# A long convolution by DFT matmuls and an MLP on one core: LayerNorm moved into the forward transform, keys and values multiplied out of PSUM, squares and diagonals spread over engines

## The chip, the core and the metric

The kernel runs on one core of a Trainium2 chip. The core has a matrix engine (TensorE, "PE" in the profile), a vector engine (VectorE, "DVE"), an activation engine (ScalarE, "ACT"), GpSimd ("POOL") and a sync engine (SyncE, "SP") that here only issues DMAs. Matmuls write into PSUM, which has eight banks; a tile of 128x512 float32 fills one. The metric is the device time of the launch in microseconds (us).

## The reference, cut to what matters

```python
def A(q, k, v, shift_k, ssm_k, ssm_D):              # S = 2048, D = 512
    k_shift = sum(k delayed by t * shift_k[:, 3 - t] for t in range(4))   # written short
    kv = k_shift * v
    y = irfft(rfft(kv, 2S) * rfft(ssm_k, 2S))[:S]    # causal convolution along S, per channel
    y = y + kv * ssm_D
    return q * y

def B(x, w1, w2, w3, w4):                            # F = 1792
    h = gelu(layernorm(x) @ w1)
    hs = (four quarters of h, shifted by +1, -1, +2, -2 along S) @ w2
    x1 = x + hs
    return x1 + gelu(layernorm(x1) @ w3) @ w4

x = A_q
h = x + A(layernorm(x), A_k, A_v, A_shift_k, A_ssm_k, A_ssm_D)
out = h + B(layernorm(h), w1, w2, w3, w4)
```

All inputs and the output are bfloat16.

## The kernel before

Most tiles hold a transposed activation: 128 partitions of channels, DC = 4 groups of channels, S = 2048 positions. NB = 16 blocks of 128 positions, NW = 4 windows of 512 positions.

The convolution is done with cosine and sine matrices that the kernel makes itself. `gen_trig` makes them: three VectorE instructions for the angle, folded into one turn, and three on ScalarE.

```python
def gen_trig(pool, x0, g, j0, cw, out_sin, out_cos, gmax):
    e = pool.tile([P, gmax, cw], F32, tag="ge");  t = pool.tile([P, gmax, cw], F32, tag="gt")
    ...
    nc.vector.tensor_tensor(out=ev, in0=bj_b, in1=rv_b, op=MUL)                 # L107
    nc.vector.tensor_scalar(out=tv, in0=ev, scalar1=MAGIC, scalar2=MAGIC, op0=ADD, op1=SUB)  # L108
    nc.vector.tensor_tensor(out=tv, in0=ev, in1=tv, op=SUB)                     # L110
    nc.scalar.activation(out_sin, tv, ACT.Sin, scale=TWO_PI)                    # L111
    nc.scalar.activation(ev, tv, ACT.Abs)                                       # L112
    nc.scalar.activation(out_cos, ev, ACT.Sin, bias=halfpi, scale=-TWO_PI)      # L113
```

LayerNorm over channels (which lie on partitions): sums and sums of squares by matmuls with a column of ones, then 1/std and -mean/std per position are put on diagonals (`dga`, `dgb`), spread over all partitions by a matmul with a matrix of ones, copied out of PSUM, and applied. It is called for q ("qn"), for h with two outputs ("hn") and for x1 ("ln1").

```python
def layernorm_feat(xt, yt, name, yt2=None):
    ...
    lps = ...tile_pool(bufs=2, space=PSUM)
    sq = lq.tile([P, DC, S], BF16)
    nc.vector.tensor_tensor(out=sq[:], in0=xt[:], in1=xt[:], op=MUL)            # L121
    pst = lps.tile([P, NB, 2], F32, bufs=1)
    for blk in range(NB):
        for c in range(DC): matmul(pst[:, blk, 0:1], lhsT=xt[:, c, blk], rhs=ones_col)   # L126
        for c in range(DC): matmul(pst[:, blk, 1:2], lhsT=sq[:, c, blk], rhs=ones_col)   # L129
    nc.scalar.mul(stat, pst, 1.0 / D)                                           # L132
    ...                                        # variance, square root (L139), rstd, brow
    for (acol, bcol, ydst) in scales:
        for w in range(NW):
            psbc = lps.tile([P, 1024], F32)
            for j in range(4):
                nc.vector.tensor_scalar_mul(dga, ident, acol[:, blk:blk + 1])   # L163, dga: 2 buffers
                nc.vector.tensor_scalar_mul(dgb, ident, bcol[:, blk:blk + 1])   # L165, dgb: 2 buffers
                matmul(psbc[:, j * P:(j + 1) * P], lhsT=ones_pp, rhs=dga)       # L166
                matmul(psbc[:, 512 + j * P:512 + (j + 1) * P], lhsT=ones_pp, rhs=dgb)   # L168
            nc.scalar.copy(abc, psbc[:, 0:512]);  nc.scalar.copy(bbc, psbc[:, 512:1024])  # L172, L173
            for c in range(DC):
                nc.vector.tensor_tensor(out=tn, in0=xt[:, c, lo:hi], in1=abc, op=MUL)     # L177
                nc.vector.tensor_tensor(out=ydst[:, c, lo:hi], in0=tn, in1=bbc, op=ADD)   # L178
```

The front loads k and v transposed, shifts k, multiplies, and transposes the product back block by block:

```python
kT = kvg.tile([P, DC, S], BF16);  vT = kvg.tile([P, DC, S], BF16)
for c in range(DC): nc.sync.dma_start_transpose(kT[:, c, :], A_k[0, :, c * P:(c + 1) * P])     # L203
for c in range(DC): nc.scalar.dma_start_transpose(vT[:, c, :], A_v[0, :, c * P:(c + 1) * P])   # L205
for c in range(DC):
    nc.vector.tensor_scalar_mul(ksh, kT[:, c, :], ssk[:, c, 0:1])               # L208
    for j in range(1, 4): nc.vector.scalar_tensor_tensor(out=ksh[:, j:], ...)   # L210
    nc.vector.tensor_tensor(out=kvTc, in0=ksh, in1=vT[:, c, :], op=MUL)         # L214
    for b in range(NB):
        pt = psK.tile([P, P], BF16)
        nc.tensor.transpose(pt, kvTc[:, b * P:(b + 1) * P], ident)              # L217
        (nc.scalar.copy if b % 2 == 0 else nc.vector.tensor_copy)(kv_all[:, b, c * P:(c + 1) * P], pt)  # L220, L222
for lb in range(NB): nc.sync.dma_start_transpose(hf[:, lb, :], A_ssm_k[...])     # L225
for c in range(DC): nc.sync.dma_start_transpose(xT[:, c, :], A_q[...])           # L228
layernorm_feat(xT, qnT, "qn")
gen_trig(..., nyq_s, nyq)
```

The forward transform has 16 chunks of 128 frequencies and one last frequency. Four spectra (real and imaginary of kernel and of kv), each with two PSUM buffers of one bank, are summed over the 16 blocks, copied out and combined into `Qr`, `Qi`:

```python
for ci, (f0, cw) in enumerate(fchunks):
    cs, ss = ...                                       # gen_trig, one chunk of 128 columns, 2 buffers
    akr, aki, ghr, ghi = four psA tiles
    for b in range(NB):
        matmul(ghr, lhsT=cs[:, b], rhs=hf[:, b]);  matmul(akr, lhsT=cs[:, b], rhs=kv_all[:, b])   # L258, L259
        matmul(ghi, lhsT=ss[:, b], rhs=hf[:, b]);  matmul(aki, lhsT=ss[:, b], rhs=kv_all[:, b])   # L260, L261
    nc.scalar.copy(acr, akr); ... aci, gcr, gci        # L266 to L269
    ...                                                # 8 VectorE instructions: Qr[:, q], Qi[:, q]
```

The inverse transform runs over four windows; the strips of sines come in groups of four frequency blocks:

```python
for w in range(NW):
    yps = psI.tile([P, DC, 512], F32)                  # four banks, 2 buffers
    for qg in range(0, NB, GQ):                        # GQ = 4
        iss, ics = its tiles (2 buffers);  gen_trig(itf, qg, GQ, lo, 512, iss, ics, GQ)
        for qi in range(GQ):
            for c in range(DC):
                matmul(yps[:, c], lhsT=Qr[...], rhs=ics[:, qi])    # L319
                matmul(yps[:, c], lhsT=Qi[...], rhs=iss[:, qi])    # L321
    ...                                                # last frequency, L324
    for c in range(DC):
        nc.vector.tensor_tensor(out=ty, in0=yps[:, c], in1=qnT[:, c, lo:hi], op=MUL)   # L328
        nc.vector.tensor_tensor(out=hT[:, c, lo:hi], in0=ty, in1=xT[:, c, lo:hi], op=ADD)   # L330
```

Then come the LayerNorms of h, the matmuls with w1 and w2 (whose results x1T are written channel group by channel group, L386), the LayerNorm of x1, and the MLP with w3 and w4 window by window.

Of the kernel before, what the change touches and what calls it, by code (L numbers as in the profile page):

```python
# [34 lines left out]
def kernel(  # L35
# [79 lines left out]
    def layernorm_feat(xt, yt, name, yt2=None):  # L115
        with ExitStack() as lctx:
            lp = lctx.enter_context(tc.tile_pool(name=f"lnp_{name}", bufs=2))
            lq = lctx.enter_context(tc.tile_pool(name=f"lnq_{name}", bufs=1))
            lps = lctx.enter_context(tc.tile_pool(name=f"lps_{name}", bufs=2, space=bass.MemoryType.PSUM))
            sq = lq.tile([P, DC, S], BF16, tag="sq")  # L120
            nc.vector.tensor_tensor(out=sq[:], in0=xt[:], in1=xt[:], op=MUL)  # L121
# [35 lines left out]
            for (acol, bcol, ydst) in scales:  # L157
                for w in range(NW):
                    psbc = lps.tile([P, 1024], F32, tag="psbc")
                    for j in range(4):  # L160
                        blk = 4 * w + j
                        dga = lp.tile([P, P], BF16, tag="dga")
                        nc.vector.tensor_scalar_mul(dga[:], ident[:], acol[:, blk:blk + 1])  # L163
                        dgb = lp.tile([P, P], BF16, tag="dgb")
                        nc.vector.tensor_scalar_mul(dgb[:], ident[:], bcol[:, blk:blk + 1])  # L165
                        nc.tensor.matmul(psbc[:, j * P:(j + 1) * P], lhsT=ones_pp[:, :],  # L166
                                         rhs=dga[:], start=True, stop=True)
                        nc.tensor.matmul(psbc[:, 512 + j * P:512 + (j + 1) * P], lhsT=ones_pp[:, :],  # L168
                                         rhs=dgb[:], start=True, stop=True)
# [11 lines left out]
    nyq_s = pI.tile([1, 1, S], BF16)  # L181

    with ExitStack() as pa_ctx:
# [12 lines left out]
        with ExitStack() as kvctx:  # L196
            kvg = kvctx.enter_context(tc.tile_pool(name="kvg", bufs=1))
            kvt = kvctx.enter_context(tc.tile_pool(name="kvt", bufs=1))
            psK = kvctx.enter_context(tc.tile_pool(name="psK", bufs=2, space=bass.MemoryType.PSUM))
            kT = kvg.tile([P, DC, S], BF16)  # L200
            vT = kvg.tile([P, DC, S], BF16)
            for c in range(DC):
                nc.sync.dma_start_transpose(kT[:, c, :], A_k[0, :, c * P:(c + 1) * P])  # L203
            for c in range(DC):
                nc.scalar.dma_start_transpose(vT[:, c, :], A_v[0, :, c * P:(c + 1) * P])  # L205
            for c in range(DC):
                ksh = kvt.tile([P, S], BF16, tag="ksh")
# [5 lines left out]
                kvTc = kvt.tile([P, S], BF16, tag="kvTc")  # L213
                nc.vector.tensor_tensor(out=kvTc[:], in0=ksh[:], in1=vT[:, c, :], op=MUL)  # L214
                for b in range(NB):
                    pt = psK.tile([P, P], BF16, tag="pt")
                    nc.tensor.transpose(pt[:], kvTc[:, b * P:(b + 1) * P], ident[:])  # L217
                    eng = nc.scalar if (b % 2 == 0) else nc.vector
                    if eng is nc.scalar:
                        nc.scalar.copy(kv_all[:, b, c * P:(c + 1) * P], pt[:])  # L220
                    else:
                        nc.vector.tensor_copy(kv_all[:, b, c * P:(c + 1) * P], pt[:])  # L222
# [7 lines left out]
        layernorm_feat(xT, qnT, "qn")  # L230
        with ExitStack() as ny_ctx:
            nyp = ny_ctx.enter_context(tc.tile_pool(name="nyp", bufs=1))
            gen_trig(nyp, NB, 1, 0, S, nyq_s[0:1, 0:1, :], nyq[0:1, 0:1, :], 1)
# [3 lines left out]

        for ci, (f0, cw) in enumerate(fchunks):
            if ci == 0:
                cs, ss = cs_pre, ss_pre  # L240
            else:
                cs = strips.tile([P, NB, CW], BF16, tag="cs")
                ss = strips.tile([P, NB, CW], BF16, tag="ss")
                gen_trig(tmpf, 0, NB, f0, cw, ss[:, :, :cw], cs[:, :, :cw], NB)
            if cw > 1:
                nq = cw // P
                for qi in range(nq):
                    q = f0 // P + qi
                    akr = psA.tile([P, 512], F32, tag="akr")
                    aki = psA.tile([P, 512], F32, tag="aki")  # L250
                    ghr = psA.tile([P, 512], F32, tag="ghr")
                    ghi = psA.tile([P, 512], F32, tag="ghi")
                    for b in range(NB):
# [4 lines left out]
                        nc.tensor.matmul(ghr[:], lhsT=lhs_c, rhs=hf[:, b, :], start=st, stop=sp)  # L258
                        nc.tensor.matmul(akr[:], lhsT=lhs_c, rhs=kv_all[:, b, :], start=st, stop=sp)  # L259
                        nc.tensor.matmul(ghi[:], lhsT=lhs_s, rhs=hf[:, b, :], start=st, stop=sp)  # L260
                        nc.tensor.matmul(aki[:], lhsT=lhs_s, rhs=kv_all[:, b, :], start=st, stop=sp)  # L261
                    acr = combp.tile([P, 512], BF16, tag="acr")
                    aci = combp.tile([P, 512], BF16, tag="aci")
                    gcr = combp.tile([P, 512], BF16, tag="gcr")
                    gci = combp.tile([P, 512], BF16, tag="gci")
                    nc.scalar.copy(acr[:], akr[:])  # L266
                    nc.scalar.copy(aci[:], aki[:])
                    nc.scalar.copy(gcr[:], ghr[:])
                    nc.scalar.copy(gci[:], ghi[:])  # L269
# [16 lines left out]
            else:  # L286
                akr = psA.tile([P, 512], F32, tag="akr")
                ghr = psA.tile([P, 512], F32, tag="ghr")
                for b in range(NB):
                    st = (b == 0)  # L290
                    sp = (b == NB - 1)
                    nc.tensor.matmul(ghr[0:1, :], lhsT=cs[:, b, 0:1], rhs=hf[:, b, :], start=st, stop=sp)
                    nc.tensor.matmul(akr[0:1, :], lhsT=cs[:, b, 0:1], rhs=kv_all[:, b, :], start=st, stop=sp)
                acr = combp.tile([P, 512], BF16, tag="acr")
                gcr = combp.tile([P, 512], BF16, tag="gcr")
                nc.scalar.copy(acr[0:1, :], akr[0:1, :])
                nc.scalar.copy(gcr[0:1, :], ghr[0:1, :])
                p1 = combp.tile([P, 512], BF16, tag="p1")
                nc.vector.tensor_tensor(out=p1[0:1, :], in0=acr[0:1, :], in1=gcr[0:1, :], op=MUL)
                nc.vector.tensor_scalar_mul(Qr[0:1, 16, :], p1[0:1, :], 1.0 / L)  # L300

    with ExitStack() as pi_ctx:
# [5 lines left out]
        GQ = 4  # L308
        for w in range(NW):
            lo, hi = w * 512, (w + 1) * 512  # L310
            yps = psI.tile([P, DC, 512], F32, tag="yps")
            for qg in range(0, NB, GQ):
                iss = its.tile([P, GQ, 512], BF16, tag="iss")
                ics = its.tile([P, GQ, 512], BF16, tag="ics")
                gen_trig(itf, qg, GQ, lo, 512, iss[:], ics[:], GQ)
# [139 lines left out]
```

## Time and profile before

| | |
|---|---|
| time, median of 4 runs | 714.63 us (713.75 to 715.33) |
| span of the profiled run | 713.4 us |
| instructions | 7378 |
| PE busy | 545.8 us (76%) |
| DVE busy | 526.8 us (74%) |
| ACT busy | 339.0 us (48%) |
| POOL busy | 2.9 us |

A busy share is a mean over stages of different kinds. The stages follow one another: the front (loads, shifted k, LayerNorm of q) until the first forward matmul at 101.2 us; the forward transform until 331; the inverse transform from 343.5 to 460.5; the LayerNorms of h until the first matmul with w1 near 507; w1 and w2 until 551.8; the LayerNorm of x1 until the first matmul with w3 near 577; the MLP to the end. In the lines of the profile "L217" is a line of the kernel, "out<-in" are tile names, and the text in brackets says how long the engine had been idle before an instruction and what released it.

### The profile page before, as it was taken

What the parts mean: (1) busy time and instruction counts of PE and PEld (TensorE: products, weight loads), DVE (VectorE), ACT (ScalarE), POOL (GpSimd) and SP (SyncE); (2) the same over time, 40 slices, a digit from 0 to 9 for tenths busy, and PEclk for the clock granted to TensorE, in tenths of its full rate; (3) what the DMA queues carried; (4) which work ended last, traced back from release to release, by engine and by line L of the source; (5) the groups of instructions that cost most, each with busy time, mean ns of one, the idle gap of its engine ahead of it and who ended that gap; (6) DMA issues with size and microseconds to landing.
All of it is one profiled execution on the core that took longest, in us unless ns stands there. A gap on an engine that the chain in (4) does not pass through costs nothing.

```text
span 713.4 us, 7378 instructions
## 1 busy us (share of the span) xinstructions
PE 545.8 (76%) x2800; PEld 245.0 (34%) x2800; DVE 526.8 (74%) x1000; ACT 339.0 (48%) x391; POOL 2.9 (0%) x11
## 2 busy tenths in 40 slices
PE   0122459999999999995799999833558468999976
PEld 0011324444444444442344444331223323433422
DVE  4699693756756665615989997179887778888984
ACT  0333417466456446512978787112470256445460
POOL 1000000000000000000000000000000000000000
PEclk9999999999999999998799999955699569999996
DMA  5646000000000000000000000070000000000000
GB/s 118 126 102 125 1 1 0 1 1 0 1 1 0 1 1 0 1 1 0 0 1 1 0 1 1 0 266 0 1 0 0 2 0 0 31 1 29 1 30 30
DMA packets 39925, 15.68 MB, mean 22 GB/s; under 512 B 34513, under 2 KB 39378, under 8 KB 39890
## 3 DMA queue, kind: packets, MB, share of 16 engines
q1 hardware_dynamic: 29234, 10.76, 6.2%
q10 hardware_dynamic: 10656, 4.46, 2.5%
q8 instruction: 22, 0.36, 0.2%
q14 instruction: 13, 0.11, 0.1%
HBM read 4.72 MB, written 2.10 MB: 10 GB/s over the span
## 4 chain that ended last, share of the span: by engine, by line
PE 57%; DVE 24%; ACT 11%; DMA 5%; issue 3%; SPq 0%; ACTq 0%; DVEq 0%
PE yps L319 8%; PE yps L321 8%; PE ghr L258 8%; PE akr L259 8%; PE ghi L260 8%; PE aki L261 8%; ACT xs L336 4%; DVE u L338 3%; PE po L412 3%; ACT sg L343 3%; DMA vT<-in_A_v_dram 2%; DVE tn L177 2%; DVE g_sb L344 2%; DVE u L339 2%; DVE ksh L210 2%
## 5 line engine op out<-in xcount | busy, mean ns | idle before, releaser
L319 PE MATMUL yps<-ics,Qr 128*128 128x512 bf16 x256 | 98.4, 384 | 12.1 <-ACT ics L113 12.1
L112 ACT ACTIVATE e<-t 128x2048 f32<-128x2048 f32 (+2 forms) x34 | 63.0, 1854 | 80.3 <-DVE t L110 79.9
L321 PE MATMUL yps<-iss,Qi 128*128 128x512 bf16 x256 | 98.3, 384 | 0.0
L260 PE MATMUL ghi<-hf,ss 128*128 128x512 bf16 x240 | 91.1, 380 | 0.0
L261 PE MATMUL aki<-kv_all,ss 128*128 128x512 bf16 x240 | 91.0, 379 | 0.0
L258 PE MATMUL ghr<-hf,cs 128*128 128x512 bf16 x240 | 91.0, 379 | 0.0
L259 PE MATMUL akr<-kv_all,cs 128*128 128x512 bf16 x240 | 91.0, 379 | 0.0
L107 DVE TENSOR_TENSOR e<-bj,rv 128x2048 f32<-128x2048 f32 (+2 forms) x34 | 75.7, 2226 | 16.6 <-ACT cs L113 11.8
L110 DVE TENSOR_TENSOR t<-e,t 128x2048 f32<-128x2048 f32 (+2 forms) x34 | 75.8, 2228 | 1.0
L412 PE MATMUL po<-g_sb,w_sb 128*128 128x512 bf16 x224 | 63.8, 391 | 9.2 <-DVE g_sb L344 5.6
L217 PE MATMUL pt<-ident,kvTc 128*128 128x128 bf16 x64 | 14.1, 275 | 62.6 <-DVE kvTc L214 29.8
L405 PE MATMUL pg<-ln1T,w_sb 128*128 128x512 bf16 x224 | 58.3, 394 | 3.6 <-ACT bbc L173 1.2
L272 DVE TENSOR_TENSOR p<-acr,gcr 128x512 bf16<-128x512 bf16 x16 | 6.8, 425 | 71.1 <-ACT acr L266 56.4
L343 ACT ACTIVATE sg<-u 128x512 bf16<-128x512 bf16 x72 | 45.2, 631 | 24.6 <-DVE u L341 23.0
L166 PE MATMUL psbc<-dga,ones_pp 128*128 128x128 bf16 x64 | 17.2, 269 | 44.8 <-DVE dga L163 44.8
L336 ACT CAST xs<-pg 128x512 bf16<-128x512 f32 x56 | 32.6, 583 | 36.4 <-DVE g_sb L344 20.9
L108 DVE TENSOR_SCALAR t<-e 128x2048 f32<-128x2048 f32 (+2 forms) x34 | 40.6, 1194 | 1.9
L113 ACT ACTIVATE ics<-e,halfpi 128x2048 bf16<-128x2048 f32 x16 | 32.0, 2003 | 20.7 <-PE yps L319 20.7
L338 DVE TENSOR_TENSOR u<-xs 128x512 bf16<-128x512 bf16 x72 | 30.5, 423 | 13.7 <-ACT xs L336 13.0
L321 PEld LDWEIGHTS <-Qi 128*128 128x128 bf16 x256 | 25.3, 99 | 42.4 <-DVE t L110 11.9
L319 PEld LDWEIGHTS <-Qr 128*128 128x128 bf16 x256 | 25.3, 99 | 32.5 <-issue 3.3
L405 PEld LDWEIGHTS <-w_sb 128*128 128x128 bf16 x224 | 22.2, 99 | 37.9 <-issue 17.8
(124 smaller groups left out, 836.8 us busy)
## 6 DMA issues: line engine op xcount, KB each, us to landing
out_dram<-osb SPq DMA_DIRECT2D x16, 128.0 KB, 1.8
w_sb<-in_B_w_dram SPq DMA_DIRECT2D x1, 1792.0 KB, 8.6
w_sb<-in_B_w_dram ACTq DMA_DIRECT2D x1, 1792.0 KB, 15.2
w_sb<-in_B_w_dram SPq DMA_DIRECT2D x1, 512.0 KB, 12.5
w_sb<-in_B_w_dram ACTq DMA_DIRECT2D x1, 512.0 KB, 16.1
hf<-in_A_ssm_k_dram SPq DMA_TRANSPOSE x16, 2.7
vT<-in_A_v_dram ACTq DMA_TRANSPOSE x4, 4.2
kT<-in_A_k_dram SPq DMA_TRANSPOSE x4, 4.2
```

The source lines that it names most:

```text
L107: nc.vector.tensor_tensor(out=ev, in0=bj_b, in1=rv_b, op=MUL)
L110: nc.vector.tensor_tensor(out=tv, in0=ev, in1=tv, op=SUB)
L112: nc.scalar.activation(ev, tv, ACT.Abs)
L258: nc.tensor.matmul(ghr[:], lhsT=lhs_c, rhs=hf[:, b, :], start=st, stop=sp)
L259: nc.tensor.matmul(akr[:], lhsT=lhs_c, rhs=kv_all[:, b, :], start=st, stop=sp)
L260: nc.tensor.matmul(ghi[:], lhsT=lhs_s, rhs=hf[:, b, :], start=st, stop=sp)
L261: nc.tensor.matmul(aki[:], lhsT=lhs_s, rhs=kv_all[:, b, :], start=st, stop=sp)
L319: nc.tensor.matmul(yps[:, c, :], lhsT=Qr[:, q, c * P:(c + 1) * P], rhs=ics[:, qi, :], start=(q == 0), stop=False)
L321: nc.tensor.matmul(yps[:, c, :], lhsT=Qi[:, q, c * P:(c + 1) * P], rhs=iss[:, qi, :], start=False, stop=False)
L343: nc.scalar.activation(sg[:], u[:], ACT.Sigmoid)
L405: nc.tensor.matmul(pg[:], lhsT=w3_sb[:, k, k2 * P:(k2 + 1) * P], rhs=ln1T[:, k, lo:hi], start=(k == 0), stop=(k == DC - 1))
L412: nc.tensor.matmul(po[:], lhsT=w4_sb[:, k2, m * P:(m + 1) * P], rhs=g_sb[:, k2, :], start=(k2 == 0), stop=(k2 == FC - 1))
```

## The change

It has eight parts. (1) v is no longer loaded transposed; it is loaded in its own layout, block by block, and the shifted k is transposed on TensorE and multiplied by v as it leaves PSUM. That takes four transposing loads and the evicting copies away. (2) The LayerNorm of q moves from ahead of the forward transform to chunk 6 of it, so that it can run beside matmuls; its PSUM pool gets one buffer, to fit. (3) To make room in PSUM the forward transform does the spectra of the kernel (`gh`) first and those of kv (`ak`) after them, each a tile of two banks, two in all. (4) The first strip of the inverse transform is made at the end of the forward stage into tiles of its own. (5) The squares of the LayerNorms are cut into pieces of 512 columns, and (6) those of h, except the last window, go to GpSimd. (7) `dgb` is made on ScalarE. (8) The last frequency's unused sine tile `nyq_s` goes; sine and cosine are written to one tile.

```diff
-            lps = ...tile_pool(name=f"lps_{name}", bufs=2, space=PSUM)
+            lps = ...tile_pool(name=f"lps_{name}", bufs=(1 if name == "qn" else 2), space=PSUM)
             sq = lq.tile([P, DC, S], BF16, tag="sq")
-            nc.vector.tensor_tensor(out=sq[:], in0=xt[:], in1=xt[:], op=MUL)
+            for w in range(NW):
+                for c in range(DC):
+                    eng = nc.gpsimd if (name == "hn" and w < NW - 1) else nc.vector
+                    eng.tensor_tensor(out=sq[:, c, w * 512:(w + 1) * 512], in0=xt[:, c, w * 512:(w + 1) * 512],
+                                      in1=xt[:, c, w * 512:(w + 1) * 512], op=MUL)
 ...
-                        nc.vector.tensor_scalar_mul(dgb[:], ident[:], bcol[:, blk:blk + 1])
+                        nc.scalar.mul(dgb[:], ident[:], bcol[:, blk:blk + 1])
 ...
-    nyq_s = pI.tile([1, 1, S], BF16)
+    GQ = 4
+    iss0 = pI.tile([P, GQ, 512], BF16)
+    ics0 = pI.tile([P, GQ, 512], BF16)
 ...
+            vtp = kvctx.enter_context(tc.tile_pool(name="vtp", bufs=3))
-            vT = kvg.tile([P, DC, S], BF16)
-            for c in range(DC):
-                nc.scalar.dma_start_transpose(vT[:, c, :], A_v[0, :, c * P:(c + 1) * P])
 ...                                            # ksh as before, but one tile for each c (kshs)
-                nc.vector.tensor_tensor(out=kvTc[:], in0=ksh[:], in1=vT[:, c, :], op=MUL)
-                for b in range(NB): ...        # transpose of kvTc, copy to kv_all
+            for b in range(NB):
+                vt = vtp.tile([P, D], BF16, tag="vt")
+                nc.scalar.dma_start(vt[:], A_v[0, b * P:(b + 1) * P, :])
+                pt = psK.tile([P, DC, P], BF16, tag="pt")
+                for c in range(DC):
+                    nc.tensor.transpose(pt[:, c, :], kshs[c][:, b * P:(b + 1) * P], ident[:])
+                nc.vector.tensor_tensor(out=kv_all[:, b, :], in0=pt[:, :, :], in1=vt[:, :], op=MUL)
 ...
-        layernorm_feat(xT, qnT, "qn")
 ...
+            if ci == 6 and not qn_done:
+                layernorm_feat(xT, qnT, "qn")
+                qn_done = True
 ...                                            # akr, aki, ghr, ghi: two tiles of two banks, tag "spec", bufs=2
+                    gh = psA.tile([P, 2, 512], F32, tag="spec")
+                    for b in range(NB): ...    # gh[:, 0] (cs), gh[:, 1] (ss) with hf
+                    nc.scalar.copy(gcr[:], gh[:, 0, :]);  nc.scalar.copy(gci[:], gh[:, 1, :])
+                    ak = psA.tile([P, 2, 512], F32, tag="spec")
+                    for b in range(NB): ...    # ak[:, 0] (cs), ak[:, 1] (ss) with kv_all
+                    nc.scalar.copy(acr[:], ak[:, 0, :]);  nc.scalar.copy(aci[:], ak[:, 1, :])
 ...
+        gen_trig(tmpf, 0, GQ, 0, 512, iss0[:], ics0[:], GQ)
 ...
-                iss = its.tile(...);  ics = its.tile(...);  gen_trig(itf, qg, GQ, lo, 512, iss[:], ics[:], GQ)
+                if w == 0 and qg == 0:
+                    iss, ics = iss0, ics0
+                else:
+                    iss = its.tile(...);  ics = its.tile(...);  gen_trig(itf, qg, GQ, lo, 512, iss[:], ics[:], GQ)
```

## The prediction

> **What bounds the kernel now.** I read the page first: busy shares and the 40 slices.
>
> ```profile
> PE 545.8 (76%) x2800; PEld 245.0 (34%) x2800; DVE 526.8 (74%) x1000; ACT 339.0 (48%) x391; POOL 2.9 (0%) x11
> ...
> PE   0122459999999999995799999833558468999976
> PEld 0011324444444444442344444331223323433422
> DVE  4699693756756665615989997179887778888984
> ```
>
> TensorE and VectorE are both near three quarters, and they take turns. The row of PE is 9 in two long blocks (the two transforms) and low in the first six slices and in slices 27 to 34, where the row of DVE is high. So I cut the span at the ends of the stages and asked for busy time in each stretch (columns: stretch, length, busy PE, PEld, DVE, ACT, POOL with counts, clock, DMA share, GB/s).
>
> ```profile
> 0.00:102.00 102.00, 24.24 (x227) 13.44 (x228) 78.93 (x135) 29.51 (x52) 2.73 (x9) 1.00 0.41 83
> 102.00:331.00 229.00, 229.00 (x1054) 102.83 (x1053) 134.84 (x179) 116.31 (x112) 0.00 (x0) 1.00 0.00 1
> 331.00:344.00 13.00, 0.93 (x4) 0.34 (x3) 12.42 (x9) 7.33 (x6) 0.00 (x0) 0.62 0.00 0
> 344.00:460.50 116.50, 116.41 (x528) 51.12 (x526) 94.73 (x67) 84.06 (x45) 0.00 (x0) 0.98 0.00 1
> 460.50:511.00 50.50, 18.67 (x201) 11.12 (x202) 43.54 (x146) 11.07 (x22) 0.14 (x2) 0.53 0.28 94
> 511.00:551.80 40.80, 28.31 (x122) 11.55 (x121) 33.10 (x80) 19.28 (x32) 0.00 (x0) 0.99 0.00 0
> 551.80:581.00 29.20, 12.94 (x169) 7.99 (x169) 22.15 (x71) 6.73 (x13) 0.00 (x0) 0.57 0.01 1
> ```
>
> The reader is to see: a front of 102 us with VectorE busy 79; a forward transform of 229 us in which TensorE never stops while VectorE has 94 us free; a hole of 13 us; an inverse transform with TensorE full again; and two LayerNorms of 50 and 29 us with VectorE busy most of the time and TensorE at a little over half clock. Work that leaves the front or the LayerNorms, or moves under the forward transform, is worth its whole length; work taken off VectorE inside the transforms is worth nothing by itself.
>
> The waits tell what ends the front (waiter, releaser: us, times, longest):
>
> ```profile
> PE pt L217 <- DVE kvTc L214: 29.8, 4, 21.2
> ...
> PE ghr L258 <- ACT bbc L173: 1.5, 1, 1.5
> ...
> SPq L203 <- DMA vT<-in_A_v_dram: 23.1, 4, 6.6
> ```
>
> The first forward matmul (L258, at 101.2 in the timeline) waits for the last copy of the LayerNorm of q (L173), although it needs nothing of it: it needs the banks of PSUM that this LayerNorm held. The queue of SyncE waits for transposing loads of vT from the other queue: kT and vT go strictly in turns.
>
> Between the stages, the hole and the statistics:
>
> ```profile
> PE yps L319 <- ACT ics L113: 12.1, 1, 12.1
> ...
> 465.37 4.42 DVE L121 TENSOR_TENSOR sq<-hT 128x8192 bf16<-128x8192 bf16 x1
> ...
> 473.36 0.20 ACT L132 ACTIVATE stat<-pst 128x32 f32<-128x32 f32 x1 [24.04 <-PE pst L129]
> ...
> 551.79 4.43 DVE L121 TENSOR_TENSOR sq<-x1T 128x8192 bf16<-128x8192 bf16 x1
> ```
>
> The inverse waits 12.1 us for its first strip of sines. One square of 8192 columns holds up each LayerNorm for 4.4 us before the sums of squares can begin.
>
> **What the Trainium skill says.** "DMA: Bandwidth & Descriptors", Rules for kernel authors: transposes on different queues must be serialized, and a transpose beside ordinary DMAs needs nothing. The trace agrees on the first half (23.1 us of waits, above); the second is what the plain loads of v rely on, and no line of this trace shows it. "VectorE: DVE Perf Modes", the perf-mode tier table: tensor_tensor runs 2x on bf16 in SBUF, 1x with an operand in PSUM. The trace agrees: 420 ns for 128x512 from SBUF (L177), 688 ns with one operand in PSUM (L415). "SBUF — State Buffer", Who interferes with whom: a VectorE instruction with two SBUF inputs and a GpSimd instruction that reads SBUF exclude each other for a whole instruction. GpSimd does nothing in these stages here, so no line shows it. "GPSIMD Engine Reference", Performance versus the Vector engine: a two-input tensor_tensor of 2048 fp32 takes 4497 ns; a quarter of that is my estimate for 512 columns, 1.1 us.
>
> **Front.** Removed: the four transposing loads of v, so the four of k need no turns (4.2 us each now, and the fourth is issued only at 30.72). VectorE's idle 5.7 us at 24.6 to 30.4, behind a ScalarE that stood issuing vT until 28.4, goes as well. Left for VectorE until kv_all is whole: four times 0.74 + 3 x 2.34 = 7.8 us, 31 us; constants 2.8; the sines of chunk 0, 2.3 + 1.2 + 2.3 = 5.8; those of chunk 1, which may be slipped in, 5.8. The 4 products (1.2 each) and 32 evictions (0.2 each) go; 16 products out of PSUM at 0.69 come, 11.0. Sum 56.4 busy; consecutive instructions overlap by about 0.07 us, so some 53. Start when the first kT lands, at about 6. The v tiles have three buffers; a plain transfer took 1.8 us to land (out) or 2.4 (shift_k), so three tiles per 2.0 + 0.7 + 0.3 is 1.0 us per block, 16 us for the 16 blocks rather than 11; the sines of chunk 1 fit in that gap. So kv_all is complete near 60. The square (4.4) and the rest of the LayerNorm of q (79.9 to 101.2) no longer stand ahead of the forward matmuls. Forward starts at 60 instead of 101: **minus 41 us**.
>
> **Forward.** The matmuls are the same 1024 + 32, 0.216 us apart. The spectra now share two slots of two banks: after gh, 6.9 us of ak pass before its slot is needed again, and two copies of 0.6 us must be done by then; that fits. The LayerNorm of q now sits inside, at chunk 6. On TensorE it adds 128 statistics matmuls at 0.027 (3.4) and 32 broadcasts at 0.06 (1.9), 5 us. On VectorE it adds about 5.4 for squares, 2.6 for dga and 10.7 for products, 19 us. VectorE has 13.8 - 9.5 = 4.3 us free per chunk and runs more than a chunk ahead (the sines of chunk 3 are begun at 123.95, while chunk 1 runs), so most is absorbed; I allow 4 us for TensorE standing in line for dga, dgb or the single psbc. **Plus 9 us.**
>
> **Inverse.** The first strip is ready in advance; it keeps TensorE for 32 x 0.216 = 6.9 us, but the second strip's buffers still lie over the forward stage's, so its chain starts as late as now. Of 12.1 us, 5 to 6 stay: minus 7. Against that: in one window VectorE needs 4 x 5.8 + 8 x 0.6 = 28.1 us of TensorE's 28.7, and the 12 squares on GpSimd, if each shuts VectorE out for 1.1 us, add 4.5 per window: 13 us at most, of which the lead of two strips and the shorter start swallow most. I allow plus 3. **Minus 4 us.**
>
> **LayerNorms of h and x1.** For h, three quarters of the squares are done during the inverse, and the last four (0.34 each) follow the last hT; the statistics of the earlier blocks run meanwhile. Instead of 465.4 + 4.4 + 3.5 to 473.4, statistics end near 467.9: **minus 5.5**. For x1, squares of 0.34 fill the 0.17 to 0.25 us gaps between the x1T additions; one or a few stay exposed: **minus 4**. Moving dgb to ScalarE takes 0.163 x 4 = 0.65 us per window off VectorE in twelve exposed windows (7.8 us), but the products then wait for the chain dga, broadcast, copy (about 1.3 us per window), which those instructions only filled: **minus 1**.
>
> Sum: -41 + 9 - 4 - 5.5 - 4 - 1 = -46.5; 714.6 - 46.5 = **668 us**.
>
> **Rivals.** (1) The new LayerNorm starves the forward transform: its 19 us on VectorE have priority over the sines of the next chunk, and TensorE waits in order for psbc with one buffer. For: ScalarE already waits 79.7 us for L110 in the forward stage. Against: the idle 94 us and the lead of a chunk. It would give 15 us more, near 683. (2) GpSimd becomes the brake of the inverse: every square blocks VectorE fully. For: VectorE is 96% busy from 360 to 440. Against: only 12 instructions, and 17.9 us of idle time before the end. It would add 8 to 10, near 677. (3) The front becomes bound by the loads of v: three buffers and issuing from ScalarE, which also computes sines of 1.9 us. If each load waits for one, kv_all comes at 70: 678. (4) All goes well, dgb included, and forward starts at 55: 652.
>
> **Range and chances.** The front's gain is the sum of VectorE's work and hardly depends on luck; even with rivals 1 and 2 both at full size the time is 692. To lose the 2% mark (700.3), 32 us would have to go wrong. Range 652 to 690. Faster 0.94, within 2% 0.04, slower 0.02.
>
> **What would show it.** Right: the first forward matmul near 60, waiting for the last product out of PSUM; no transposing load on ScalarE's queue; TensorE at 9 from there to the end of the forward stage, which is some 235 us long; a hole of 5 to 6 us after the first 32 inverse matmuls; stat of h within 8 us of the last inverse matmul. Wrong: holes in PE around chunks 6 to 8 named dga, dgb or ss/cs; VectorE's L107 or L110 lengthened or waiting in the inverse with POOL busy beside them; a forward start later than 70.

## The result, and the profile after

The changed kernel takes 675.99 us (median, 674.83 to 677.75), the kernel before 714.96 in the same runs: a ratio of 0.9458, 95% interval 0.9447 to 0.9468. The prediction was 668 (652 to 690). The profiled execution lasts 673.8 us, that of before 713.4. Line numbers from here on are those of the kernel named.

The page of the kernel after: the rows of TensorE (busy 80% of the span, 76% before), VectorE (76%, 74% before) and GpSimd over 40 slices.

```profile
PE   0024999999999999997999999633668389999976
...
DVE  5998576557966555569999995469888789888975
...
POOL 1000000000000000000040403000000000000000
```

TensorE reaches 9 in the fifth slice instead of the seventh, the notch between the transforms is a 7, and GpSimd has work in three windows of the inverse. The same cut by stages as before, at the new ends of the stages (stretch, length, busy PE, PEld, DVE, ACT, POOL with counts, clock, DMA share, GB/s):

```profile
0.00:64.80 64.80, 9.21 (x69) 7.11 (x70) 55.40 (x51) 15.38 (x9) 2.73 (x9) 1.00 0.60 130
64.80:304.40 239.60, 237.10 (x1212) 107.69 (x1212) 152.41 (x245) 134.67 (x143) 0.00 (x0) 1.00 0.00 1
304.40:316.40 12.00, 7.08 (x33) 3.14 (x33) 11.91 (x9) 6.30 (x5) 0.00 (x0) 0.92 0.00 0
316.40:428.00 111.60, 110.51 (x496) 48.27 (x495) 95.43 (x63) 79.56 (x42) 20.59 (x12) 0.98 0.00 1
428.00:472.00 44.00, 15.02 (x193) 10.20 (x194) 33.70 (x108) 21.24 (x52) 0.14 (x2) 0.53 0.33 108
...
516.00:538.50 22.50, 10.97 (x161) 7.57 (x161) 18.34 (x63) 11.49 (x27) 0.00 (x0) 0.57 0.01 1
```

Read from the first and last matmul of each stage in the two timelines (w1 and w2 end with the last x1T addition), that makes this ledger (us):

| stage | before | after | difference | predicted |
|---|---|---|---|---|
| front, up to the first forward matmul | 101.2 | 64.8 | -36.4 | -41 |
| forward transform | 230.2 | 239.6 | +9.4 | +9 |
| inverse transform, with the hole ahead of it | 129.0 | 123.6 | -5.4 | -4 |
| LayerNorm of h, to the first w1 matmul | 47.0 | 44.0 | -3.0 | -5.5 |
| the two matrix stages (w1, w2) | 44.3 | 44.1 | -0.2 | 0 |
| LayerNorm of x1, to the first w3 matmul | 25.6 | 22.2 | -3.4 | -4 |
| the rest | 136.1 | 135.5 | -0.6 | 0 |

The prediction's last -1, for dgb on ScalarE, lies in the two LayerNorm rows. The waits of TensorE in the transforms, kernel after (waiter, releaser: us, times, longest):

```profile
PE gh L261 <- ACT cs L113: 2.4, 6, 0.4
PE gh L261 <- DVE kv_all L225: 0.5, 1, 0.5
...
PE yps L335 <- ACT ics L113: 4.3, 1, 4.3
PE yps L337 <- ACT iss L111: 1.1, 1, 1.1
```

The front now ends with the last product of k and v (L225) and no longer with the LayerNorm of q, and the inverse waits 4.3 us where it waited 12.1. A second wait of 1.1 us, for the last strip of the last window, is new (run 8). The timeline after the inverse shows what the prediction had not seen:

```profile
435.39 0.20 ACT L136 ACTIVATE stat<-pst 128x32 f32<-128x32 f32 x1 [15.26 <-PE pst L133]
435.39 5.13 ACTq L379 DMA_DIRECT2D w_sb<-in_B_w_dram  x1
...
440.56 1.28 ACT L143 ACT_TABLE_LOAD   x1 [4.98 <-issue]
...
515.97 5.45 DVE L124 TENSOR_TENSOR sq<-x1T 128x512 bf16<-128x512 bf16 x16
```

The statistics of h are there 7.4 us after the last inverse matmul (427.99), 5.5 sooner than before. But then ScalarE stands for 5 us on the issue of the load of w2, and the square root comes after it. And all sixteen squares of x1 still come in one block after the last x1T.

### The profile page after: what moved, and what is told of

It reads as the page before. It is cut to its first block, busy times and chain, and to the rows that moved or that the text cites. A ratio compares the mean times of both kernels' runs of the same rounds, so it can differ in the third digit from the quotient of the medians.

```text
span 673.8 us, 7391 instructions
## 1 busy us (share of the span) xinstructions
PE 539.3 (80%) x2800; PEld 244.2 (36%) x2800; DVE 513.1 (76%) x949; ACT 353.9 (53%) x422; POOL 23.5 (3%) x23
## 4 chain that ended last, share of the span: by engine, by line
DVE 40%; PE 35%; ACT 17%; issue 3%; DMA 2%; SPq 1%; ACTq 1%; DVEq 0%
DVE e L107 6%; DVE t L110 6%; PE gh L261 5%; PE gh L262 5%; PE ak L274 5%; PE ak L273 5%; ACT xs L352 4%; DVE u L354 4%; DVE t L108 3%; PE po L428 3%; ACT sg L359 3%; ACT e L112 2%; DVE ksh L215 2%; PE yps L337 2%; PE yps L335 2%
## 5 line engine op out<-in xcount | busy, mean ns | idle before, releaser
L107 DVE TENSOR_TENSOR e<-bj,rv 128x2048 f32<-128x2048 f32 (+2 forms) x34 | 78.2, 2299 | 76.8 <-ACT cs L113 74.6
L261 PE MATMUL gh<-hf,cs 128*128 128x512 bf16 x240 | 91.1, 380 | 2.4 <-ACT cs L113 2.4
L273 PE MATMUL ak<-kv_all,cs 128*128 128x512 bf16 x240 | 91.1, 379 | 0.0
L262 PE MATMUL gh<-hf,ss 128*128 128x512 bf16 x240 | 91.0, 379 | 0.0
L274 PE MATMUL ak<-kv_all,ss 128*128 128x512 bf16 x240 | 91.0, 379 | 0.0
L265 ACT CAST gcr<-gh 128x512 bf16<-128x512 f32 x16 | 9.4, 585 | 66.3 <-PE gh L262 66.3
L108 DVE TENSOR_SCALAR t<-e 128x2048 f32<-128x2048 f32 (+2 forms) x34 | 42.4, 1248 | 1.3
L421 PEld LDWEIGHTS <-w_sb 128*128 128x128 bf16 x224 | 22.1, 99 | 37.5 <-issue 17.2
L428 PEld LDWEIGHTS <-w_sb 128*128 128x128 bf16 x224 | 21.2, 99 | 39.7 <-issue 23.6
```

Source lines behind the costliest of these rows:

```text
L261: nc.tensor.matmul(gh[:, 0, :], lhsT=lhs_c, rhs=hf[:, b, :], start=st, stop=sp)
L262: nc.tensor.matmul(gh[:, 1, :], lhsT=lhs_s, rhs=hf[:, b, :], start=st, stop=sp)
L273: nc.tensor.matmul(ak[:, 0, :], lhsT=lhs_c, rhs=kv_all[:, b, :], start=st, stop=sp)
L274: nc.tensor.matmul(ak[:, 1, :], lhsT=lhs_s, rhs=kv_all[:, b, :], start=st, stop=sp)
L421: nc.tensor.matmul(pg[:], lhsT=w3_sb[:, k, k2 * P:(k2 + 1) * P], rhs=ln1T[:, k, lo:hi], start=(k == 0), stop=(k == DC - 1))
L428: nc.tensor.matmul(po[:], lhsT=w4_sb[:, k2, m * P:(m + 1) * P], rhs=g_sb[:, k2, :], start=(k2 == 0), stop=(k2 == FC - 1))
```

## The experiments

The theory: each part works by the mechanism that the prediction gave; what is missing is at the end of the front, behind the load of w2, and in the squares of x1. Every time below is to be compared with 676.0 us of the kernel after.

**1. The LayerNorm of q ahead of the forward stage again.**

```
+        layernorm_feat(xT, qnT, "qn")          # behind the loads of xT
-        qn_done = False
+        qn_done = True
```

> The kernel after, with the LayerNorm of q put back ahead of the forward transform; everything else as after (676.0 us). Theory (the move takes VectorE work out of a front that VectorE bounds, and TensorE pays half of it back inside the forward stage): first forward matmul at about 86 instead of 64.8, forward stage about 230 instead of 239.6, so 676 + 21 - 10 = 687. Rival (the front was bound by the path of v, and the LayerNorm of q could fill VectorE's gaps there): first forward matmul within 8 us of 64.8, forward stage 230, time 674 or less.

Measured: 696.62 us, ratio to before 0.9752 (0.9718 to 0.9786). The first forward matmul, by its group in the trace (count, shortest/median/longest ns, first and last start):

```profile
L262 PE MATMUL gh<-hf,cs_pre x16: 379/380/632, 91.5 to 100.8; 128*128 128x512 bf16 x16
```

The front is 26.7 us longer, the forward stage (91.5 to 327.1) only 4.0 shorter. The rival falls. So does the size in the theory: the forward stage did not come back to 230. At its second chunk TensorE waits 3.0 us for the copy gci, since ScalarE put the sines of the last frequency (the Nyquist row) and one strip of the next chunk ahead of the copies, and after that wait seven more matmuls come about 0.43 us apart instead of 0.216 (1.4 us). The thirteen matmuls 0.43 us apart at its start explain little of the difference: the kernel before has ten of them, the kernel after nine. From this run alone I took the LayerNorm's cost inside to be 5 to 6 us, which run 3 refutes.

**2. The old way of v, with the LayerNorm of q still inside.** Four transposing loads of v on ScalarE's queue, kvTc, and 64 transposes with copies, as in the kernel before.

```
-                vt = vtp.tile(...);  nc.scalar.dma_start(vt[:], A_v[0, b * P:(b + 1) * P, :])
+                nc.scalar.dma_start_transpose(vT[:, c, :], A_v[0, :, c * P:(c + 1) * P])
+                nc.vector.tensor_tensor(out=kvTc[:], in0=ksh[:], in1=vT[:, c, :], op=MUL)
```

> The kernel after, with v loaded by four transposing loads and multiplied before the transposes of TensorE, as in the kernel before; the LayerNorm of q stays inside the forward stage. Theory (turns between the transposing loads, and more work for VectorE: four products of 1.2 and 32 evictions of 0.2 against sixteen products of 0.41): first forward matmul between 76 and 82, time 688 to 694. Rival (nearly all of the front's gain is the LayerNorm's move, v's path is hidden behind the loads of hf and x): first forward matmul under 70, time under 681.

Measured: 717.81 us, ratio 1.0045 (1.0032 to 1.0059): slower than the kernel before, far outside both expectations. The first forward matmul starts at 106.2. Its timeline says why:

```profile
58.61 0.16 PE L130 MATMUL pst<-ones_col,xT 128*128 128x1 bf16 x1 [27.14 <-DMA xT<-in_A_q_dram]
```

The compiler had slipped the first statistics matmuls of the LayerNorm (L130) in among the transposes of k times v. TensorE takes its instructions in order, x is loaded last (its issues begin at 53.39), and so the transposes, and VectorE behind them, stood for 27 us. In the kernel after the same matmuls stand there too (27.1 us for xT), but its transposes would have waited for the fourth ksh anyway. So this run does not measure the path of v alone. Run 4 does.

**3. The LayerNorm of q left out.** The output is another one; q itself takes its place in the inverse.

```
-        qn_done = False
+        qn_done = True
-                                        in1=qnT[:, c, lo:hi], op=MUL)
+                                        in1=xT[:, c, lo:hi], op=MUL)
```

> The kernel after, with the LayerNorm of q left out altogether (q itself, transposed, takes its place in the product of the inverse); the output is another one. It measures what this LayerNorm still costs where it now lies. Prediction's view (9 us on TensorE and in waits inside the forward stage): forward stage 230, time 667. Theory from the run with the LayerNorm in front (forward stage 235.2, of which 3 us half clock at its start and 3 us a wait at its second chunk): the LayerNorm costs 5 to 6 us inside, forward stage 234, time 670. Rival (it is hidden but for its 5 us of matmuls on TensorE, and these too fill gaps): 673 or more.

Measured: 665.35 us, ratio 0.9306 (0.9291 to 0.9321). The two ends of the forward stage, by groups:

```profile
L261 PE MATMUL gh<-hf,cs_pre x16: 379/379/631, 64.4 to 72.7; 128*128 128x512 bf16 x16
...
L304 PE MATMUL gh<-kv_all,cs x16: 379/379/379, 290.8 to 294.0; 128*1 128x512 bf16 x16
```

From 64.4 to 294.4, with the 0.4 us of the last matmul: 230.0 us instead of 239.6. The LayerNorm costs 9.6 us where it lies, the prediction's 9, not the 5 to 6 of my theory after run 1. The starts of TensorE's matmuls in the kernel after say where nearly all of it goes: 3.1 us for the matmuls of the statistics, 2.7 for the broadcasts with the little that they wait, and 3.6 at the heads of seven later chunks, where the sines come late. At six of these the next gh starts 0.78 us after the last ak instead of 0.216 (the 2.4 us of waits for cs above are the idle part of that). None of it is left in this run.

**4. The old way of v, with the LayerNorm of q left out.** Runs 2 and 3 together.

> The kernel of before's way with v (four transposing loads, products before TensorE's transposes), with the LayerNorm of q left out as in the run that measured its cost inside (665.4 us), so that no statistics matmul stands in TensorE's order ahead of the transposes. Output differs as there. Theory (v's new path is worth turns of the queues and VectorE's work): first forward matmul at 78 to 82 instead of 64.4, time 679 to 683. Rival 1 (the long stand on statistics was only a part, the old path of v is itself as slow as 100): time over 695. Rival 2 (v's path is worth little): time under 671.

Measured: 680.29 us, ratio 0.9513 (0.9499 to 0.9528), 14.9 above run 3.

```profile
L264 PE MATMUL gh<-hf,cs_pre x16: 379/379/631, 78.5 to 87.5; 128*128 128x512 bf16 x16
```

The first forward matmul starts at 78.5. Counted from this side, the path of v is worth 78.5 - 64.4 = 14.1 us of the front's 36.4, and the LayerNorm's departure the other 22.3. Counted from run 1 it is 101.2 - 91.5 = 9.7 for the path and 26.7 for the departure, so the split depends on which comes first. The move as it is written needs the new path: without it, it is run 2, slower than the kernel before, because of where the statistics matmuls came to stand.

**5. w2 loaded by SyncE.**

```
-            nc.scalar.dma_start(w2_sb[:], B_w2.rearrange("(k p) o -> p k o", p=P))
+            nc.sync.dma_start(w2_sb[:], B_w2.rearrange("(k p) o -> p k o", p=P))
```

> The kernel after, with the load of w2 issued by SyncE instead of ScalarE; nothing else. Theory (in the LayerNorm of h the square root stands behind 5 us in which ScalarE issues this load, so the statistics' gain of 5.5 was given back): den follows stat within 2 us, first w1 matmul 5 us earlier after the inverse's end, time 671. Rival (the load of the table of functions or a wait for w2 itself takes its place): time 675 to 676.

Measured: 671.45 us, ratio 0.9394 (0.938 to 0.9409): 4.5 faster than the kernel after. ScalarE's timeline (the issue of w2 now takes SyncE 2.04 us):

```profile
436.72 0.20 ACT L136 ACTIVATE stat<-pst 128x32 f32<-128x32 f32 x1 [15.26 <-PE pst L133]
...
438.23 0.31 ACT L143 ACTIVATE den<-varr,eps_t 128x16 f32<-128x16 f32 x1
```

The square root starts 1.5 us after stat instead of 6.5. The stage shrinks from 44.0 to 39.0. The theory holds.

**6. dgb on VectorE again.**

```
-                        nc.scalar.mul(dgb[:], ident[:], bcol[:, blk:blk + 1])
+                        nc.vector.tensor_scalar_mul(dgb[:], ident[:], bcol[:, blk:blk + 1])
```

> The kernel after, with the second diagonal (dgb) made by VectorE again in all three LayerNorms. Theory from the trace after (the eight windows of the LayerNorm of h take 31.9 us instead of 34.1, and the four of x1 about 1 us less): time 679. The prediction's view (the move is worth 1 us, since the products wait for the broadcast and its copies anyway): 677. Rival (ScalarE, with dgb and the copies on one engine, is the slower part of the chain): 674 or less.

Measured: 680.85 us, ratio 0.9525 (0.9511 to 0.954): 4.9 slower. The LayerNorms of h and x1 in stretches as above:

```profile
429.10:475.30 46.20, 14.90 (x192) 9.73 (x193) 37.63 (x141) 10.48 (x20) 0.15 (x2) 0.53 0.31 103
519.90:543.80 23.90, 10.64 (x161) 7.31 (x161) 20.24 (x79) 6.08 (x11) 0.00 (x0) 0.58 0.01 2
```

They are 2.2 and 1.7 us longer than in the kernel after, with 3.9 and about 2 us more of VectorE. So half and more of VectorE's relief is gained: its time is the bound there, more than the chain from diagonal to copy. The remaining 1.0 came ahead of the inverse and is not shown to be dgb's: in runs that leave the LayerNorm of q as it is (5, 7, 8, 11) the forward stage lies between 239.7 and 241.1, too. So dgb is worth about 4, and the prediction's 1 us is too small.

**7. The first strip of the inverse made in the inverse.**

```
-                if w == 0 and qg == 0:
+                if False:                       # and no gen_trig(tmpf, ..., iss0, ics0) at the end of the forward stage
```

> The kernel after, with the first strip of sines of the inverse made in the inverse stage again, as in the kernel before. Theory (the strip made in advance keeps TensorE for 32 matmuls, and then the second strip is waited for): the hole of 4.3 + 1.1 us after the first strip becomes one of about 12 us ahead of it, time 676 + 7 = 683. Rival (the strip made in advance only shifts the wait, since the chain of strips has its own pace of about 6 us each on VectorE): time 676 to 678.

Measured: 683.48 us, ratio 0.9549 (0.9536 to 0.9562): 7.5 slower. TensorE's wait:

```profile
PE yps L334 <- ACT ics L113: 12.1, 1, 12.1
```

The wait of before is back, whole, and the inverse takes 130.6 us instead of 123.6. The strip is worth its 7 us.

**8. The squares of h on VectorE.**

```
-                    eng = nc.gpsimd if (name == "hn" and w < NW - 1) else nc.vector
+                    eng = nc.vector
```

> The kernel after, with the twelve squares of h that GpSimd makes during the inverse made by VectorE in the same places. Theory (the GpSimd squares cost nothing where they lie, and VectorE has a lead of 13.7 us at the end of the inverse, of which 12 x 0.35 = 4.2 us would go): time within 1 us of 676, hn statistics as far after the inverse's end as in the kernel after (7.4 us). Rival 1 (squares on GpSimd slow VectorE by sharing, so the inverse gets shorter): 674 or less. Rival 2 (VectorE is the bound of the inverse, the squares taken off it are what keeps TensorE full): 680 or more.

Measured: 675.35 us, ratio 0.9438 (0.9425 to 0.9451), against 0.9447 to 0.9468 of the kernel after: 0.6 lower, with intervals that overlap. Neither rival stands as a time. But the timelines at the first window's end differ. First the kernel after, GpSimd and then VectorE:

```profile
342.72 2.36 POOL L124 TENSOR_TENSOR sq<-hT 128x512 bf16<-128x512 bf16 x2 [339.43 <-DVE hT L346]
345.70 4.47 POOL L124 TENSOR_TENSOR sq<-hT 128x512 bf16<-128x512 bf16 x2 [0.63 <-DVE hT L346]
...
344.30 1.93 DVE L346 TENSOR_TENSOR hT<-ty,xT 128x512 bf16<-128x512 f32 x2
346.15 3.12 DVE L107 TENSOR_TENSOR e<-bj,rv 128x2048 f32<-128x2048 f32 x1
349.38 1.87 DVE L108 TENSOR_SCALAR t<-e 128x2048 f32<-128x2048 f32 x1
```

and VectorE with the squares on it:

```profile
344.82 1.28 DVE L346 TENSOR_TENSOR hT<-ty,xT 128x512 bf16<-128x512 f32 x2
346.02 2.28 DVE L107 TENSOR_TENSOR e<-bj,rv 128x2048 f32<-128x2048 f32 x1
348.23 0.42 DVE L124 TENSOR_TENSOR sq<-hT 128x512 bf16<-128x512 bf16 x1
348.56 1.22 DVE L108 TENSOR_SCALAR t<-e 128x2048 f32<-128x2048 f32 x1
```

GpSimd's squares lengthen VectorE's instructions by 0.65, 0.84 and 0.65, 2.1 us in a window; the four squares on VectorE itself take 4 x 0.34 = 1.4 between starts. GpSimd took nothing off VectorE: it cost it more. TensorE pays a little for it. Its wait of 1.1 us for iss, for the last strip of the inverse, is gone in this run, as it was absent in the kernel before, while every profile with GpSimd's squares has it. The inverse takes 121.5 us instead of 123.6 (of the 2.1, 1.2 are this wait; 0.7 are fewer matmuls at half pace after the first strip). The time hardly shows it, because the forward stage, which this edit does not touch, came out 1.5 us longer in this profile. So rival 1 has the mechanism right and its size too large. VectorE's 13.7 us of idle time at the end come after its last strip; they do not help the strip.

**9. The Nyquist row inside the forward stage.**

```
-        with ExitStack() as ny_ctx: ...  gen_trig(nyp, NB, 1, 0, S, nyq..., nyq..., 1)
+            if ci == 2:
+                with ExitStack() as ny_ctx: ...  gen_trig(nyp, NB, 1, 0, S, nyq..., nyq..., 1)
```

> The kernel after, with the row of sines for the Nyquist frequency made inside the forward stage, at the third chunk, instead of ahead of it. Theory (VectorE took it, 5.7 us, ahead of the last products of k and v, and VectorE bounds the front): first forward matmul at 59 to 60.5 instead of 64.8, forward stage unchanged, time 670 to 671.5. Rival (loads of v with their three buffers are the bound of the last products, and the row only filled the gaps): first forward matmul after 62.5, time 674 or more.

Measured: 675.3 us, ratio 0.9436 (0.9424 to 0.9449). The first forward matmul comes at 63.5, 1.3 sooner, which is the rival. VectorE's products:

```profile
56.31 0.80 DVE L225 TENSOR_TENSOR kv_all<-pt,vt 128x512 bf16<-128x512 bf16 x2 [1.12 <-DMA vt<-in_A_v_dram]
...
60.46 2.28 DVE L107 TENSOR_TENSOR e<-bj,rv 128x2048 f32<-128x2048 f32 x1
```

The products now wait for the three buffers of v, and the compiler filled the room with the sines of a later chunk (60.46). The first kT also landed 1.0 us later in this profile (8.16 instead of 7.18), so counted from there the row's move brings 2.3. Two bounds of nearly equal length lie here.

**10. v without rotating buffers, and the Nyquist row inside.** v is loaded straight into kv_all and multiplied in place.

```
+                nc.scalar.dma_start(kv_all[:, 4 * g:4 * g + 4, :],       # g = 0..3, first on ScalarE's queue
+                                    A_v[0, g * 512:(g + 1) * 512, :].rearrange("(b p) d -> p b d", p=P))
-                nc.vector.tensor_tensor(out=kv_all[:, b, :], in0=pt[:, :, :], in1=vt[:, :], op=MUL)
+                nc.vector.tensor_tensor(out=kv_all[:, b, :], in0=pt[:, :, :], in1=kv_all[:, b, :], op=MUL)
```

> The kernel after, with v loaded straight into the place of the product (four loads of four blocks, issued at the start, no rotating buffers, product in place) and the Nyquist row made inside the forward stage. Moving the row alone brought nothing. Theory (two bounds of equal length lay on the end of the front: VectorE's work and the three buffers of v, whose next loads ScalarE issues between its sines; both must go): first forward matmul at 57 to 59, forward stage unchanged at 240, time 668.5 to 670.5. Rival 1 (the plain loads slow the transposing loads of k beside them): first product of k later by several us, gain under 3. Rival 2 (the slower start of TensorE's clock, or strips of sines that are now late, swallow it): first matmul at 58, but time 673 or more.

Measured: 676.49 us, ratio 0.9467 (0.9452 to 0.9481): no gain. VectorE's first instruction on k:

```profile
15.36 0.75 DVE L215 TENSOR_SCALAR ksh<-kT,ssk 128x2048 bf16<-128x2048 bf16 x1 [11.14 <-DMA kT<-in_A_k_dram]
```

Rival 1, and stronger than I thought: with 2 MB of v on ScalarE's queue from 0.74 us on, VectorE gets the first kT 8.2 us later (15.36 instead of 7.18), and SyncE's four issues of k take 18.5 us instead of 10.3. From the first kT to the first forward matmul it is now 66.6 - 15.4 = 51.2 us instead of 57.6: the theory's gain is there, and k's delay eats it.

**11. The squares of x1 in memory of their own.**

```
+        sq1 = pB.tile([P, DC, S], BF16)                       # beside x1T, ahead of the matrix stages
-            layernorm_feat(x1T, ln1T, "ln1")
+            layernorm_feat(x1T, ln1T, "ln1", sq=sq1)
```

> The kernel after, with the squares of x1 (ahead of the last LayerNorm) in memory of their own that is set apart before the two matrix stages, instead of in memory that those stages still hold. Theory (the squares could not start before the last x1T addition because of that memory; free of it, they fill VectorE's gaps between the additions): statistics of x1 ready 3.5 to 4 us after the last addition instead of 6.4, time 672 to 673. Rival (the additions themselves leave no gap that holds a square, the squares then delay them): time 675 or more.

Measured: 674.09 us, ratio 0.9432 (0.9419 to 0.9445): 1.9 faster, half of what was expected. VectorE's timeline:

```profile
513.45 1.49 DVE L404 TENSOR_TENSOR x1T<-pw,hnT 128x512 bf16<-128x512 f32 x2
514.85 0.75 DVE L125 TENSOR_TENSOR sq<-x1T 128x512 bf16<-128x512 bf16 x2
```

The squares do lie among the additions now, and statistics come 3.7 us after the last addition (6.4 in the kernel after). But the squares push the additions: from first to last start they take 15.7 us instead of 14.9. The memory was what held the squares; the gaps were too small for them.

**12. The four edits that answer to losses, together.** w2 on SyncE (run 5), own memory for the squares (11), the Nyquist row inside (9), and v straight into kv_all, now on SyncE's queue behind k. As built, the order of that queue is k, x, v, impulse response, so x comes ahead of v and not behind it as the expectation says.

```
+            for c in range(DC): nc.sync.dma_start_transpose(xT[:, c, :], ...)     # all behind the loads of kT
+            for g in range(4):  nc.sync.dma_start(kv_all[:, 4 * g:4 * g + 4, :], ...)
+            for lb in range(NB): nc.sync.dma_start_transpose(hf[:, lb, :], ...)
```

> The kernel after with four edits: the load of w2 issued by SyncE, the squares of x1 in memory of their own, the Nyquist row inside the forward stage, and v loaded straight into the place of the product, this time on SyncE's queue behind the loads of k (then x, then the impulse response), so that k is not held up. Theory (the earlier try with v delivered k 8.2 us late and still lost only 2 us at the first forward matmul; with k on time it starts at 57 to 60): 676 - 6 (front) - 4.5 (w2, measured) - 1.9 (squares, measured) = 663.5, range 661 to 666. Rival (the impulse response, now last, holds up the forward transform, or the statistics matmuls stand for x): first forward matmul at 63 or later, time 668 or more.

Measured: 661.45 us, ratio 0.9247 (0.9234 to 0.926), 14.5 under the kernel after. VectorE's start on k in its timeline, and the first forward matmuls as a group:

```profile
6.98 0.75 DVE L220 TENSOR_SCALAR ksh<-kT,ssk 128x2048 bf16<-128x2048 bf16 x1 [3.75 <-DMA kT<-in_A_k_dram]
```

```profile
L263 PE MATMUL gh<-hf,cs_pre x16: 379/379/631, 58.1 to 66.2; 128*128 128x512 bf16 x16
```

k is on time again, and the forward stage starts at 58.1, 6.7 sooner than in the kernel after. From the first kT to there VectorE idles only 1.1 us, in four waits for transposes. So VectorE's own work is the floor of the front, and what lay on top of it was the Nyquist row and the waits for v (x's earlier place in the queue changed with them and was not tried alone).

## Why the prediction was right, and where its sum was off

**What bounds the kernel.** The reading held: work that left the front or the LayerNorms came off the time, and squares moved off VectorE in the inverse brought nothing (run 8).

**Front, -41, measured -36.4.** The mechanism held, and both halves are needed (runs 1 to 4). Start at 60 was 64.8, the sum of four terms. VectorE starts at 7.2, not about 6 (+1.2). The sixteen products out of PSUM took 0.41 us each, not 0.69 (about -4.4). The Nyquist row was forgotten (+5.7): the step listed the sines of chunks 0 and 1 alone, and the compiler placed the row among the products as well. And the waits for v and for transposes at the end cost some 2.5, which the step had covered with the sines of chunk 1. That makes 5.0, against 4.8 measured. It was luck that the products, taken too high, hid most of the row that was forgotten. Runs 9, 10 and 12 show the last two terms as a pair: the row's move alone brings 1.3, both bring 6.7 (new buffers for v alone were not tried).

The rate of the products was misread from these lines, the first two of the kernel before, the third of the kernel after:

```profile
L415 DVE TENSOR_TENSOR tf<-po,x1T 128x512 f32<-128x512 f32 x16 | 10.7, 688 | 1.4 <-PE po L412 1.1
L417 DVE TENSOR_TENSOR fb<-tf,hT 128x512 bf16<-128x512 f32 x16 | 10.6, 684 | 0.0
50.28 0.41 DVE L225 TENSOR_TENSOR kv_all<-pt,vt 128x512 bf16<-128x512 bf16 x1
```

The prediction laid the 688 ns of L415 on PSUM. But L417, whose fp32 operand lies in SBUF, takes 684: it is the type that costs, and the new products read bf16. The Trainium skill, "VectorE: DVE Perf Modes", puts tensor_tensor with any operand in PSUM at 1x in its perf-mode tier table; its section Why PSUM operands drop a tier keeps 1x for fp32 alone and allows twice that rate otherwise. The 0.41 us agree with the section and not with the table's row.

**Forward, +9, measured +9.4.** Right in size: 9.6 are the LayerNorm (run 3). The small matmuls, with what the broadcasts wait, took 5.8 where 5 were predicted. The allowance of 4 was meant for waits for dga, dgb or psbc; hardly any came there, and 3.6 came as waits for the sines instead. That is the mechanism of rival 1 at a quarter of its 15 us.

**Inverse, -4, measured -5.4.** The strip was taken at 7 and is worth 7 in the stage, 7.5 in the time (run 7). Of the allowance of 3 for GpSimd 1.1 was needed (run 8). Its mechanism is real: the Trainium skill, "SBUF — State Buffer", Who interferes with whom, has VectorE with two SBUF inputs and GpSimd's reads share a port under an exclusive lock, and this trace agrees with a mutual brake, since a square takes 1.2 us in one pair and 2.2 in the next while three VectorE instructions, two of them with two SBUF inputs, grow by 0.65 to 0.84. But it is 2.1 us a window, not 4.5, and TensorE feels it once, at the last strip. Rival 2, 8 to 10 us more, is false.

**LayerNorm of h, -5.5, measured -3.0.** The step's own figure, statistics at 467.9 in the old count, came to within 0.1: 7.4 us after the inverse instead of 12.95. What failed is that it ended at the statistics. In the kernel before, the issue of w2 lay under the square and the sums:

```profile
465.98 6.63 ACTq L363 DMA_DIRECT2D w_sb<-in_B_w_dram  x1
```

It came out from under the work that had hidden it and took back 5.0; run 5 recovers 4.5. Without the -2.2 of dgb nearly nothing would have been gained here.

**LayerNorm of x1, -4, measured -3.4.** Right in sum, wrong in the reason: 1.8 came from the statistics running beside the squares, about 1.7 from dgb (run 6). The squares did not fill gaps, because their memory lay over the stage before; given other memory (run 11) they do, for 1.9 more.

**dgb, -1, measured about -4** (run 6). The step took the chain of diagonal, broadcast and copy as the bound of a window. It was, for the larger part, VectorE's work.

**Rivals.** 3, the loads of v, was the half-right one: not each load, but the last few, and only once the Nyquist row had gone does it become the bound. In the sum, the front (4.6) and the LayerNorm of h (2.5) fell short; dgb, hidden in the rows of the two LayerNorms, and the inverse gave back some, and 8 us remained to the measured 676.

## What to carry to other kernels

A step of a sum should not end where the shortened work ends, but at the next instruction that uses it: what was hidden under the old work (here the issue of a load on the engine that takes the square root) becomes the new wait. When one bound is removed and nothing comes, ask for a second of equal length before giving up the theory: the Nyquist row's move brought 1.3 us alone and, with v's buffers gone and the queue in the right order, 6.7. And moving a stage in an in-order program moves its small first instructions too: the two halves of the front's change are worth 36 us together, and the move alone less than nothing (run 2). Work given to another engine is not gone: GpSimd's squares cost VectorE 2.1 us a window, where VectorE would have made them in 1.4.

## What the runs showed of the hardware

- A tensor_tensor of 128x512 with one bf16 operand in PSUM and one bf16 in SBUF took 0.41 to 0.42 us, as from SBUF alone (0.42). With an fp32 operand it took 0.68 to 0.69, in PSUM (L415) and in SBUF (L417) alike.
- A square of 128x512 bf16 on GpSimd took 1.2 us beside VectorE's products out of PSUM and 2.2 beside its instructions on SBUF, which grew by 0.65 to 0.84 each.
- Issuing the 512 KB load of w2 held ScalarE for 5.1 us behind a load of 1792 KB on its own queue. The issue of that larger load took 0.46. On SyncE, behind its own loads, w2's issue took 2.0 us in run 5 and 0.5 in run 12. Why it waits is not shown.
- 2 MB of plain loads, issued on ScalarE's queue beside the transposing loads of SyncE, delayed the first of these by 8.2 us (run 10). Behind them on one queue they did not: the first kT was used at 6.98 us (run 12).
- After a stretch of little work TensorE began at half rate: 0.43 us between the first 8 to 12 large matmuls of a stage in the kernel after, then 0.216. A hole of 4.3 us was enough (after the first strip of the inverse), one of 0.7 us was not (ahead of it). The granted clock over these matmuls is 0.51 in the inverse (314.4 to 321.3). At the start of the forward stage a view prints 1.00, but there the trace has no entry of the clock before 68.7 us, the moment the spacing falls to 0.216.
